# RWKV-6 attention followed by a Hyena gate, last output product split: two blocks of y ahead, the third behind

## The chip, the cores and the metric

One core of one Trainium2 chip. Times are device microseconds. The engines are PE (matrix products), VectorE (DVE), ScalarE (ACT), GpSimd (POOL) and SyncE (SP), which here only issues DMAs; sixteen DMA engines move the data. A PE product is two instructions in the profile, a weight load (PEld) and a matmul.

## The reference

Two layers in a row, for 4 batches, 768 time steps, 8 heads of 48 (384 channels):

```
# 1: a decaying state per head
y[t]  = r[t] @ (state + (u * k[t]) outer v[t])
state = w[t] * state + k[t] outer v[t]
# 2: x = y with the heads side by side, [batch, 768, 384]
x1, x2, x3 = split(x @ w_proj)
conv = irfft(rfft(x2, time) * rfft(filter, time))
out  = (x1 * conv * x3) @ w_out
```

## The kernel before, in words

Layer 1 is done in 24 chunks of 128 time steps, six for each batch. Layer 2 is done batch by batch: the projections, a Fourier transform written as matrix products, a pointwise product with the filter's transform, the inverse transform, the gate, and the output product.

The order of the work is written out by hand. ORDER is a text of words such as `P:po.3.3@2`: the engine (P is PE, V VectorE, A ScalarE, G GpSimd, S SP), the operation with its arguments (here batch 3, tile 3), and after the @ the PSUM bank. `emit` calls `op_<name>` for each word. Within an engine, instructions go in the order of the words; between engines, only data, buffers and the marks (!) order them. There are six banks of 128 x 384 fp32 (0 to 5), and one wide one (8). A word that names a bank takes it anew (`ps`) and so waits for the last reader of what lay in it.

What the change touches is the end of each batch:

- The 384 channels are three blocks of 128 (`cb`, CB = 3), with channels on the partitions and the 768 time steps along the row. For each block the inverse transform gives two halves, which VectorE adds and subtracts into `SD_b[cb]` (`op_s` line 759, `op_d` line 768).
- `op_gm` (line 692) makes a half of the gate x1 * x3, `op_gc` copies a half of the third projection out of PSUM (line 241), `op_x1` one of the first.
- `op_yy` (line 771) multiplies: y[:, cb, :] = SD[cb] * g[:, cb, :], 128 x 768 in bf16, on VectorE or GpSimd. All three blocks lie in one tile, `y_b[0]`, the same one for all batches.
- `op_po` (line 776) is the output product for one tile of 128 time steps: three matmuls, one for each block of y, summed in one PSUM bank. There are six tiles for a batch.
- `op_o` evicts the bank into `o_b` (line 241 on ScalarE, 242 on VectorE; the tile is called `filt` in odd batches), and `op_st` (line 785) has SP store the 192 KB to HBM.

In the last batch there is nothing left beside this. The words after the last projections are: `yy.3.2` on GpSimd, then on VectorE `yy.3.0`, `gm.3.1.1`, `yy.3.1`, so block 1 is the last to be ready. PE's six `po` words follow, in banks 2, 3, 0, 2, 3, 0, with five evictions on ScalarE and one (`o.3.1`) on VectorE. The stores go in the order 3, 5, 4, 2, 0, 1.

Of the kernel before, what the change touches and what calls it, by code (L numbers as in the profile page):

```python
# [19 lines left out]
B, H, S, D = 4, 8, 768, 48  # L20
# [3 lines left out]
CB = C // L  # L24
# [104 lines left out]
S:st.2.5 V:pp.3.2 P:po.2.4@1 S:st.2.1 V:pp.3.1 P:p1.3.2.1@0 V:o.2.4 P:i2.3.2@2 V:g.3.0.1 S:st.2.4  # L129
P:i1.3.2@1 A:ec.3.2 V:x1.3.2.1 P:p3.3.2.1@3 V:d.3.2 P:i2.3.0@0 V:s.3.2 P:i1.3.0@2 A:ec.3.0 V:g.3.2.1  # L130
P:i2.3.1@1 V:s.3.0 G:yy.3.2! P:i1.3.1@3 A:ec.3.1 V:d.3.0 P:p1.3.1.1@0 V:s.3.1 P:p3.3.1.1@2
A:x1.3.1.1 V:d.3.1 A:gc.3.1.1 V:yy.3.0 V:gm.3.1.1 V:yy.3.1 P:po.3.3@2 P:po.3.5@3 A:o.3.3 P:po.3.4@0
A:o.3.5 S:st.3.3 P:po.3.2@2 A:o.3.4 S:st.3.5 P:po.3.1@3 A:o.3.2 S:st.3.4 P:po.3.0@0 V:o.3.1 S:st.3.2
A:o.3.0 S:st.3.0 S:st.3.1
"""


# [1 line left out]
def kernel(  # L139
# [90 lines left out]
    bank_of = {}  # L230

    def ps(name, bank, shape=(L, C), dt=FP32):
        t = (wide if bank == 8 else banks[bank]).tile(
            list(shape), dt, tag="a", name=name.replace(".", "_")
        )
        bank_of[name] = t
        return t
# [532 lines left out]
    def op_yy(e, b, cb):  # L770
        return two(e).tensor_mul(y_b[0][:, cb, :], SD_b[cb], g_b[b % 2][:, cb, :])  # L771

    def op_po(e, b, ti, bank):
        p = ps(f"po.{b}.{ti}", bank)
        for cb in range(CB):
            nc.tensor.matmul(  # L776
                p, y_b[0][:, cb, ti * L:(ti + 1) * L], wout[:, cb, :],
                start=(cb == 0), stop=(cb == CB - 1),
            )

    def op_o(e, b, ti):
        copy(e, o_b[b % 2][:, ti, :], bank_of[f"po.{b}.{ti}"])
# [101 lines left out]
```

## Time and profile before

| | |
|---|---|
| median of 3 runs | 159.45 us (159.06 to 159.55) |
| the profiled execution's own time | 159.7 us |
| its span, first to last instruction | 158.0 us |
| mean granted PE clock | 0.993 |
| PE, VectorE, ScalarE, GpSimd busy | 93%, 90%, 79%, 71% |
| stores of the last batch | 6 of 192 KB, issued from 151.57 to 154.84 |

All times in the text are microseconds from the start of the span. A row of the timeline gives the start, the duration, the engine and line, the operation, what it writes and reads, its count, and in brackets how long the engine stood idle before it and what ended that. SPq is the queue of SP: its duration is the time that SP is taken up with issuing, and not that of the transfer. A group's row gives durations in ns as least, median and most. A window's row gives each engine's busy time and instructions, then PE's clock, the busy share of the 16 DMA engines, and the GB/s that they moved.

### The profile page before, as it was taken

The numbers are of one execution on the slowest core, as the hardware profiler recorded it, in microseconds if no ns is written. First come the engines' busy times: TensorE is split into PE (matmuls) and PEld (weight loads), VectorE is DVE, ScalarE is ACT, GpSimd is POOL, SyncE is SP. The second block draws the span as 40 slices with busy tenths as digits, with TensorE's granted clock in tenths as the row PEclk, the third lists the DMA queues.
The fourth block names the chain that finished last, engine by engine and source line by source line (L and its number), as shares of the span: only waits on it lengthen the run. The fifth ranks groups of instructions, "written<-read, shape, count | busy, mean of one in ns | idle before, by whom it ended". The sixth has DMA issues, their size and how long they took to land.

```text
span 158.0 us, 4363 instructions
## 1 busy us (share of the span) xinstructions
PE 146.7 (93%) x1635; PEld 96.9 (61%) x1638; DVE 142.1 (90%) x287; ACT 125.6 (79%) x264; POOL 111.7 (71%) x136
## 2 busy tenths in 40 slices
PE   6999999989999999999999999999999989899770
PEld 6656467666567676767566766666667746456340
DVE  6989999985999999999998999999999999899920
ACT  4699799998889999999979999799786755644460
POOL 7373399987767888987797479887988969741400
PEclk9999999999999999999999999999999999999997
DMA  5999999999999989979899989999972000016026
GB/s 104 206 245 260 181 217 190 173 257 167 279 228 222 217 174 193 269 152 220 166 191 217 194 172 224 290 215 204 223 212 71 0 0 4 2 52 244 5 77 228
DMA packets 105704, 27.43 MB, mean 174 GB/s; under 512 B 100305, under 2 KB 105682, under 8 KB 105682
## 3 DMA queue, kind: packets, MB, share of 16 engines
q1 hardware_dynamic: 105682, 27.14, 76.9%
q8 instruction: 13, 0.21, 0.6%
q14 instruction: 9, 0.07, 0.1%
HBM read 22.41 MB, written 4.72 MB: 172 GB/s over the span
## 4 chain that ended last, share of the span: by engine, by line
PE 61%; ACT 11%; DVE 9%; POOL 8%; DMA 6%; issue 2%; SPq 0%; POOLq 0%; ACTq 0%
PE p L666 12%; PE po L776 8%; DMA ldw<-in_w_dram 6%; PE x L697 5%; PE i L737 5%; PE tqk L566 4%; PE f L411 4%; PE sc L579 3%; PE cs L467 2%; PE ce L473 2%; PE f L404 2%; PE y L622 2%; ACT F L344 2%; POOL vc L560 2%; POOL T L444 1%
## 5 line engine op out<-in xcount | busy, mean ns | idle before, releaser
L586 DVE TENSOR_TENSOR mt<-sc,mask_excl 128x1024 bf16<-128x1024 f32 x24 | 29.2, 1215 | 0.5 <-PE sc L579 0.5
L666 PE MATMUL p<-xT,wproj 128*128 128x384 bf16 x144 | 29.3, 326 | 0.3 <-ACT xT L241 0.2
L528 POOL TENSOR_TENSOR rk<-ldr,ldk 128x384 bf16<-128x384 f32 x23 | 22.9, 999 | 6.4 <-DMA ldr<-in_r_dram 2.5
L560 POOL TENSOR_TENSOR vc<-v,cc 128x384 bf16<-128x384 bf16 x24 | 20.0, 836 | 6.1 <-DVE cc L534 1.8
L241 ACT ACTIVATE qkT<-tqk 128x1024 bf16<-128x1024 bf16 x20 | 20.5, 1032 | 3.8 <-PE tqk L566 3.8
L666 PEld LDWEIGHTS <-wproj 128*128 128x128 bf16 x144 | 13.0, 98 | 7.1 <-issue 0.3
L697 PE MATMUL x<-wproj,sd 128*128 128x384 bf16 x72 | 14.8, 326 | 1.4 <-DVE sd L653 1.1
L463 ACT ACTIVATE lg<-ldw 128x384 bf16<-128x384 f32 x24 | 12.7, 529 | 3.4 <-DMA ldw<-in_w_dram 3.2
L776 PE MATMUL po<-wout,y 128*128 128x384 bf16 x72 | 13.7, 326 | 1.2 <-DVE y L771 1.2
L566 PE MATMUL tqk<-ident,qk 128*128 128x128 bf16 x192 | 14.6, 219 | 0.1
L771 POOL TENSOR_TENSOR y<-SD,g 128x768 bf16<-128x768 bf16 x6 | 9.9, 1642 | 6.6 <-DVE g L682 4.6
L525 POOL TENSOR_TENSOR qk<-ldr,eq 128x384 bf16<-128x384 f32 x12 | 12.3, 1027 | 2.9 <-ACT eq L492 1.2
L737 PE MATMUL i<-m_b,P 128*128 128x384 bf16 x72 | 13.8, 326 | 0.3 <-DVE g L682 0.3
L566 PEld LDWEIGHTS <-qk 128*128 128x128 bf16 x192 | 11.6, 98 | 3.3 <-DVE qk L509 0.7
L241 ACT ACTIVATE ab<-x 128x384 bf16<-128x384 f32 x22 | 10.8, 497 | 3.0 <-PE x L697 3.0
L731 POOL TENSOR_TENSOR P<-UA,UB 128x768 bf16<-128x768 bf16 x5 | 8.2, 1641 | 4.5 <-DVE UB L722 2.8
L521 POOL TENSOR_TENSOR qk<-ldk,en 128x384 bf16<-128x384 f32 x10 | 10.0, 1000 | 1.9 <-DVE qk L525 1.1
L605 DVE TENSOR_TENSOR S<-kv,eq 128x384 bf16<-128x384 f32 x20 | 11.0, 549 | 0.2
L241 ACT ACTIVATE x<-p 128x384 bf16<-128x384 f32 x21 | 9.9, 496 | 1.5 <-PE p L666 1.5
L776 PEld LDWEIGHTS <-y 128*128 128x128 bf16 x72 | 6.5, 98 | 5.9 <-DVE y L771 2.0
L242 POOL CAST v<-ldv 128x384 bf16<-128x384 f32 x12 | 6.5, 547 | 5.1 <-DVE UA L393 4.6
L634 DVE TENSOR_TENSOR xn<-y,vc 128x384 bf16<-128x384 f32 x18 | 9.9, 548 | 0.0
(155 smaller groups left out, 411.7 us busy)
## 6 DMA issues: line engine op xcount, KB each, us to landing
ldw<-in_w_dram SPq DMA_DIRECT2D x24, 192.0 KB, 3.8
ldk<-in_k_dram SPq DMA_DIRECT2D x24, 192.0 KB, 4.0
ldr<-in_r_dram SPq DMA_DIRECT2D x24, 192.0 KB, 4.1
ldv<-in_v_dram SPq DMA_DIRECT2D x24, 192.0 KB, 4.1
out_dram<-o SPq DMA_DIRECT2D x12, 192.0 KB, 3.2
out_dram<-filt SPq DMA_DIRECT2D x12, 192.0 KB, 2.2
o<-in_moe_w_proj_dram SPq DMA_DIRECT2D x3, 576.0 KB, 5.4
filt<-in_moe_filter_fft_dram SPq DMA_DIRECT2D x1, 1152.0 KB, 7.2
```

The source lines that it names most:

```text
L241: return nc.scalar.activation(out=o, in_=i, func=AF.Copy)
L463: nc.scalar.activation(out=lg_b[c % 3][:, :, 0:D], in_=ld["w"][c % LD], func=AF.Ln)
L525: return two(e).tensor_mul(qk_b[c % 3][:, 0, :, 0:D], ld["r"][c % LD], eq)
L528: return two(e).tensor_mul(rk_b[c % 2], ld["r"][c % LD], ld["k"][c % LD])
L560: return two(e).tensor_mul(vc_b[c % 3], v_b[c % 4], cc_b[c % 3].to_broadcast([L, H, D]))
L566: nc.tensor.transpose(p[:, x, j, :], qk_b[c % 3][:, x, 2 * j:2 * j + 2, :], ident)
L586: nc.vector.tensor_mul(mt_b[c % 3], bank_of[f"sc{c}"].rearrange("p q j t -> p (q j) t"), dataclasses.replace(m[:, :], ap=[m[:, :].ap[0], [ ...
L605: nc.vector.tensor_mul(S_b[nth(c)], bank_of[f"kv{c}"], ph.to_broadcast([L, HP, 2, D]))
L666: nc.tensor.matmul(p, wproj[:, n, cb, fb * L:(fb + 1) * L], xT_b[b % 2][:, cb, sl], start=(cb == 0), stop=(cb == CB - 1),)
L697: nc.tensor.matmul(p, sd_b[q][:, cb, ti * L:(ti + 1) * L], wproj[:, 1, cb, :], start=(cb == 0), stop=(cb == CB - 1),)
L737: nc.tensor.matmul(p, P_b[b % 2][:, s // 2, s % 2, cb * L:(cb + 1) * L], m_b[:, s].rearrange("p a t -> p (a t)"), start=(i == 0), stop=(i ...
L776: nc.tensor.matmul(p, y_b[0][:, cb, ti * L:(ti + 1) * L], wout[:, cb, :], start=(cb == 0), stop=(cb == CB - 1),)
```

## The change

The three matmuls of an output tile are now taken in the order of blocks 2, 0, 1, in all batches. For the last batch the product of a tile is two words: `poa` takes a bank and issues the matmuls of blocks 2 and 0, `pob` issues that of block 1 into the same bank. The `poa` of tiles 3, 5 and 4 stand ahead of `yy.3.1` in the list and ahead of all `pob` on PE; the other three tiles have `poa` and `pob` next to each other. The six tiles take the banks 4, 5, 0, 1, 3, 2. The evictions and the stores keep their engines and their order, and are moved to the end of the list.

```diff
-A:x1.3.1.1 V:d.3.1 A:gc.3.1.1 V:yy.3.0 V:gm.3.1.1 V:yy.3.1 P:po.3.3@2 P:po.3.5@3 A:o.3.3 P:po.3.4@0
-A:o.3.5 S:st.3.3 P:po.3.2@2 A:o.3.4 S:st.3.5 P:po.3.1@3 A:o.3.2 S:st.3.4 P:po.3.0@0 V:o.3.1 S:st.3.2
-A:o.3.0 S:st.3.0 S:st.3.1
+A:x1.3.1.1 V:d.3.1 A:gc.3.1.1 V:yy.3.0 V:gm.3.1.1 P:poa.3.3@4 P:poa.3.5@5 P:poa.3.4@0 V:yy.3.1
+P:pob.3.3 A:o.3.3 P:pob.3.5 A:o.3.5 P:pob.3.4 A:o.3.4 P:poa.3.2@1 P:pob.3.2 A:o.3.2 P:poa.3.1@3
+P:pob.3.1 V:o.3.1 P:poa.3.0@2 P:pob.3.0 A:o.3.0 S:st.3.3 S:st.3.5 S:st.3.4 S:st.3.2 S:st.3.0
+S:st.3.1
...
-    def op_po(e, b, ti, bank):
-        p = ps(f"po.{b}.{ti}", bank)
-        for cb in range(CB):
+    FIRST = (2, 0, 1)
+
+    def po(b, ti, cbs):
+        p = bank_of[f"po.{b}.{ti}"]
+        for cb in cbs:
             nc.tensor.matmul(
                 p, y_b[0][:, cb, ti * L:(ti + 1) * L], wout[:, cb, :],
-                start=(cb == 0), stop=(cb == CB - 1),
-            )
+                start=(cb == FIRST[0]), stop=(cb == FIRST[-1]),
+            )
+
+    def op_po(e, b, ti, bank):
+        ps(f"po.{b}.{ti}", bank)
+        po(b, ti, FIRST)
+
+    def op_poa(e, b, ti, bank):
+        ps(f"po.{b}.{ti}", bank)
+        po(b, ti, FIRST[:2])
+
+    def op_pob(e, b, ti):
+        po(b, ti, FIRST[2:])
```

## The prediction

> **What bounds the kernel now.** I read the page first, then the timeline of the last ten microseconds, then SP's issues and the DMA windows there.
>
> ```profile
> span 158.0 us, 4363 instructions
> PE 146.7 (93%) x1635; PEld 96.9 (61%) x1638; DVE 142.1 (90%) x287; ACT 125.6 (79%) x264; POOL 111.7 (71%) x136
> ...
> PE 61%; ACT 11%; DVE 9%; POOL 8%; DMA 6%; issue 2%; SPq 0%; POOLq 0%; ACTq 0%
> ```
>
> Over the whole span PE and VectorE are nearly full, and the chain runs mostly over PE. The change moves work only behind the last pipeline stage, so the averages say little. What counts is who ends last there. The timeline columns are start, duration, engine, line, operation, tiles, count, and the idle time before it:
>
> ```profile
> 147.35 1.65 POOL L771 TENSOR_TENSOR y<-SD,g 128x768 bf16<-128x768 bf16 x1 [4.58 <-DVE g L682]
> ...
> 147.81 1.14 PE L666 MATMUL p<-xT,wproj 128*128 128x384 bf16 x6
> ...
> 149.02 0.55 DVE L771 TENSOR_TENSOR y<-SD,g 128x768 bf16<-128x768 bf16 x1
> 149.51 0.36 DVE L692 TENSOR_TENSOR g<-g,x 128x384 bf16<-128x384 bf16 x1
> ...
> 149.63 0.34 PE L776 MATMUL po<-wout,y 128*128 128x384 bf16 x1 [0.68 <-DVE y L771]
> 149.90 0.56 DVE L771 TENSOR_TENSOR y<-SD,g 128x768 bf16<-128x768 bf16 x1
> ...
> 150.52 2.94 PE L776 MATMUL po<-wout,y 128*128 128x384 bf16 x17 [0.56 <-DVE y L771]
> 151.05 1.95 ACT L241 ACTIVATE filt<-po 128x384 f32<-128x384 f32 x4 [1.58 <-PE po L776]
> ...
> 153.00 0.56 DVE L242 COPY filt<-po 128x384 f32<-128x384 f32 x1 [2.54 <-PE po L776]
> 153.49 0.49 ACT L241 ACTIVATE filt<-po 128x384 f32<-128x384 f32 x1 [0.48 <-PE po L776]
> ```
>
> The three blocks of y arrive as block 2 (POOL, 149.00), block 0 (149.57), block 1 (150.46). PE takes them as 0, 1, 2 within each of six tiles, so it gets one matmul done at 149.63 and stands until 150.52. The other 17 leave at (2.94 - 0.326)/16 = 0.163 us each, 0.326 being what one matmul takes in the trace:
>
> ```profile
> L776 PE MATMUL po<-wout,y x18: 326/326/337, 149.6 to 153.1; 128*128 128x384 bf16 x18
> ```
>
> Evictions follow at 1.95/4 = 0.488 us on ScalarE, and the last one ends at 153.98. But the span ends at 158.0, four microseconds later, so the stores must be read too:
>
> ```profile
> 151.57 0.33 SPq L785 DMA_DIRECT2D out_dram<-filt  x1
> ...
> 152.06 1.23 SPq L785 DMA_DIRECT2D out_dram<-filt  x1
> ...
> 153.38 0.87 SPq L785 DMA_DIRECT2D out_dram<-filt  x2
> ...
> 154.34 0.91 SPq L785 DMA_DIRECT2D out_dram<-filt  x2
> ```
>
> SP issues the first store 0.03 us after its eviction. The second issue holds SP for 1.23 us instead of 0.33, until 153.29; the third, whose tile was ready at about 152.52, goes at 153.38. The windows (the last two columns are the share of the 16 DMA engines and GB/s) show what that costs:
>
> ```profile
> 152.25:152.50 0.25, 0.25 (x4) 0.12 (x3) 0.00 (x0) 0.25 (x1) 0.00 (x0) 1.00 0.32 117
> 152.25:153.00 0.75, 0.75 (x7) 0.43 (x6) 0.00 (x0) 0.75 (x2) 0.00 (x0) 1.00 0.68 246
> 153.00:153.75 0.75, 0.46 (x3) 0.07 (x1) 0.56 (x1) 0.27 (x2) 0.00 (x0) 1.00 0.10 27
> 153.75:156.50 2.75, 0.00 (x0) 0.00 (x0) 0.00 (x0) 0.23 (x1) 0.00 (x0) 0.85 0.99 355
> 156.50:158.00 1.50, 0.00 (x0) 0.00 (x0) 0.00 (x0) 0.00 (x0) 0.00 (x0) 0.50 0.02 5
> ```
>
> The first store's data flows from about 152.42 (a third of the first window at the full rate), 0.85 us after its issue. From 153.00 to 153.75 the DMA engines stand almost idle. From 153.75 all 16 are full until 156.50, with five stores: 2.75/5 = 0.55 us each. Then 1.5 us of landing and closing. So the last stage is bound by the stores: five in a row, starting when SP is let go of the second.
>
> Why was SP held? The DMA view of 151.5 to 152.0, in 40 slices, shows one packet, an instruction fetch on queue q8; the third line is the page's count of such fetches:
>
> ```profile
> GB/s 0 0 0 0 1311 0 0 0 0 0 0 0 0 0 0 0 0 0 0 0 0 0 0 0 0 0 0 0 0 0 0 0 0 0 0 0 0 0 0 0
> ...
> q8 instruction: 1, 0.02, 17.0%
> ...
> q8 instruction: 13, 0.21, 0.6%
> ```
>
> It starts in the fifth slice, 151.55, just before the first store, and takes 17% of 16 engines in 0.5 us, which on one engine is 0.17 x 16 x 0.5 = 1.36 us, to 152.91. The second issue ends 0.38 us behind that. The 0.10 of the engines busy after 153.00 is little more than one engine of 16 (0.06), which fits one engine doing its part of the first store late. Thirteen fetches over 1635 + 1638 records make one per 252 matmuls and weight loads: I read q8 as PE's own instruction stream, fetched by PE's progress. That reading is an inference.
>
> **The change part by part.**
>
> *Order of blocks (2, 0, 1), all batches.* Same 72 matmuls. Only a stall on y could change, and in the list of waits PE's output product waits for y twice in all, both in the rows above:
>
> ```profile
> PE po L776 <- DVE y L771: 1.2, 2, 0.7
> ```
>
> So batches 0 to 2 are costed at nothing: PE's earlier work covers y there, and if that cover were thinner the new order would wait no later than the old, since every order ends with the last block.
>
> *Six matmuls ahead.* Block 2 of the first tile can go at about 149.05, when POOL and PE's preceding product (147.81 + 1.14 = 148.95) are done. Block 0 goes at 149.63 as now, and four more behind it: the sixth has left by 149.63 + 5 x 0.163 = 150.44. Block 1 still comes at 150.46, so the next matmul goes at 150.52 as now, with 0.08 us of standing in place of 0.56. Then 12 are left instead of 17: PE ends 5 x 0.163 = 0.81 us sooner, at 152.65 instead of 153.46.
>
> *Banks.* The six tiles lie in six banks instead of reusing three, and banks 4 and 5 must be free. Bank 5's last reader before is VectorE's product on f.3.2, bank 4's comes ahead of it in VectorE's order; the last readers of the others are ScalarE's:
>
> ```profile
> 141.57 0.96 DVE L725 TENSOR_TENSOR UA<-f,T 128x768 bf16<-128x768 f32 x1
> ...
> 148.56 0.49 ACT L241 ACTIVATE x<-p 128x384 bf16<-128x384 f32 x1 [0.54 <-PE p L666]
> 148.99 0.49 ACT L241 ACTIVATE g<-p 128x384 bf16<-128x384 f32 x1
> ```
>
> All are done before 149.5, and bank 2 (the g row) is taken only by the last tile: no wait added.
>
> *Evictions.* The first needs one matmul after block 1 instead of two: 151.05 - 0.16 = 150.89. ScalarE then runs without a gap, because PE is ahead of it: four by 150.89 + 1.95 = 152.84, the last 152.84 to 153.33, against 153.98. So 0.65 of PE's 0.81 arrives here; ScalarE has become late next. VectorE's one eviction (ninth matmul after 150.52) ends at about 152.75, ahead of its store.
>
> *Stores.* Same six, same order on SP; nothing is moved past them. The first issue goes at 151.57 - 0.16 = 151.41, its data at 152.26. If SP is not held, issues follow every 0.49 us and data every 0.55, so the engines never run dry: 152.26 + 6 x 0.55 = 155.56 against 156.50, a gain of 0.94. If SP is held exactly as now, only 0.16.
>
> *The fetch.* At 151.55 PE has started its eighth matmul (150.52 + 6 x 0.163 = 151.50). With the change the eighth goes at 150.52 + 0.16 = 150.68, so the fetch moves to about 150.73 and ends at 152.09. The second issue comes at 151.90; with the same 0.38 behind the fetch it ends at 152.47, its data starts 0.46 later (as 153.29 to 153.75) at 152.93, and five stores end at 155.68: gain 0.82. Free of it 0.94. There is a smaller fetch in the window from 153.5 to 154.0:
>
> ```profile
> q14 instruction: 1, 0.01, 4.7%
> ```
>
> That is 0.047 x 16 x 0.5 = 0.37 us on one engine, so far partly inside the idle stretch. If it now falls among the full stores it costs up to 0.37; nothing if its engine has slack. I keep 0.45 to 0.94 and take 0.8, near the upper end, since the rows give 0.82 and only part of the small fetch is new.
>
> The Trainium skill (Runtime: NRT & Kernel Launch, Instruction fetch mechanics) says that instructions come in blocks of 16 KiB, 256 instructions, and that crossing such a block is mostly hidden. The size agrees with 0.21 MB in 13 fetches; were the cost hidden here too, the hold would have another cause and the first rival below would hold. The Trainium skill (DMA: Bandwidth & Descriptors, Queues, rings and completion order) says that a DMA engine changes queues only at packet boundaries; by that rule one 16 KB packet blocks its engine for its whole 1.36 us, as the thin stretch after 153.00 suggests.
>
> Sum: the profiled execution took 159.7 with a span of 158.0; 0.8 less is 158.9. The median of the three runs is 0.25 below that execution, so I forecast 159.45 - 0.8 = 158.65.
>
> **The rivals.**
>
> *The hold stays.* If the 1.23 us belong to the second store and not to the fetch, or the fetch does not follow PE, SP is held as now and the gain is the 0.16 of the first eviction: 159.3. In between, a fetch that moves by half as much leaves 0.3 to 0.5. For it: one instance only. Against it: six stores of the batch before had no such issue,
>
> ```profile
> L785 SPq DMA_DIRECT2D out_dram<-o x6: 332/332/341, 140.5 to 144.8; - x6
> ```
>
> 332 to 341 ns, each. Chance 0.24.
>
> *No head start.* If the write of block 1 is made to wait for the six reads of the same tile of y, it runs from about 150.65 (150.28 + 0.33 and a semaphore) to 151.21, the first eviction comes at about 151.63, 0.58 later than now. PE's eighth matmul then goes at about 151.43, and with its fetch 0.07 sooner than now SP is let go 0.07 sooner: 159.4. Against it: the matmul at 149.63 read block 0 of that tile 0.83 us before block 1 was written, so blocks are told apart at least in that direction. Chance 0.07.
>
> *The fetch lands among the stores: slower.* The place of the fetch goes by a count of instructions, and the new waits may shift that count. Ten matmuls further on, behind the last of the 18 (152.32), it would block one engine for 1.36 us in the full stretch. That engine ends at 155.56 + 1.36 = 156.92, 0.42 behind now: 159.87. It decides as soon as more than 0.94 of the 1.36 fall behind 152.26. Against it: the matmuls and loads are as many as before, so ten matmuls, 20 instructions, would have to vanish. Chance 0.05.
>
> **How the numbers follow.** Forecast 0.64, and the rivals 0.24, 0.07 and 0.05. A measurement of this kernel can tell about 0.3%, 0.48 us, from no change. Faster: nearly all of the forecast (0.62) and the upper part of the first rival (0.04), 0.66. Slower: 0.05. Same: 0.29. The forecast alone reaches from 158.5 to 159.0; with 0.15 for the spread of the runs below, and the first rival above, the range is 158.35 to 159.4, which leaves out the slower case and part of the second rival.
>
> **What would show it.** Right: one matmul of the output product near 149.05, five from 149.63, twelve from 150.52; ScalarE's five evictions in one piece from 150.89; the q8 fetch near 150.7; all SP issues below 0.6 us; DMA engines full from 152.3 to 155.6 without a gap. Wrong: an issue above 1 us again with the fetch elsewhere (first rival); a VectorE write of y that starts after 150.6 (second); the fetch behind 152 (third).

## The result, and the profile after

| | before | changed |
|---|---|---|
| median of 20 runs each | 160.01 us | 158.62 us |
| ratio, 95% interval | | 0.9946 (0.992 to 0.9971) |
| profiled execution, span | 159.7, 158.0 | 158.6, 156.8 |
| mean granted PE clock | 0.993 | 0.997 |

The kernel is faster by 0.54%, between 0.29 and 0.80%: 0.9 us, with bounds of 0.5 and 1.3. The ratio leaves out the runs that took over 1.5% longer than the fastest of their kernel (of the traced executions, that of the third kernel below is one), so it is not the ratio of the two medians, which are 1.39 us apart. Runs of one kernel spread over more than two microseconds here, so most of what follows goes by the traces of the tail, one execution for each kernel.

The timeline of the changed kernel's end, with the columns as before:

```profile
146.72 1.64 POOL L772 TENSOR_TENSOR y<-SD,g 128x768 bf16<-128x768 bf16 x1 [4.58 <-DVE g L683]
...
148.40 0.55 DVE L772 TENSOR_TENSOR y<-SD,g 128x768 bf16<-128x768 bf16 x1
...
148.42 0.34 PE L780 MATMUL po<-wout,y 128*128 128x384 bf16 x1
...
149.00 3.02 PE L780 MATMUL po<-wout,y 128*128 128x384 bf16 x17 [0.25 <-DVE y L772]
149.28 0.56 DVE L772 TENSOR_TENSOR y<-SD,g 128x768 bf16<-128x768 bf16 x1
...
150.27 2.28 ACT L242 ACTIVATE filt<-po 128x384 f32<-128x384 f32 x5 [1.41 <-PE po L780]
150.78 2.79 SPq L800 DMA_DIRECT2D out_dram<-filt  x6
151.57 0.56 DVE L243 COPY filt<-po 128x384 f32<-128x384 f32 x1 [1.73 <-PE po L780]
```

One matmul goes behind POOL's block 2 and the others from block 0 on. PE stands 0.25 us for block 0 where it stood 0.68. For block 1, where it stood 0.56, it now stands 0.07: its seventh matmul starts at 149.89, 0.23 behind the sixth, and 0.16 is the usual distance. VectorE writes block 1 from 149.28 to 149.84, and doesn't wait for the reads that run beside it. ScalarE's five evictions stand in one row. SP takes 2.79 us for its six issues, where it took 3.68. The stores' group and the windows behind it:

```profile
L800 SPq DMA_DIRECT2D out_dram<-filt x6: 332/398/412, 150.8 to 153.2; - x6
```

```profile
151.75:154.95 3.20, 0.27 (x2) 0.00 (x0) 0.38 (x1) 0.65 (x2) 0.00 (x0) 1.00 0.99 354
155.00:155.50 0.50, 0.00 (x0) 0.00 (x0) 0.00 (x0) 0.00 (x0) 0.00 (x0) 1.00 0.06 22
155.50:156.80 1.30, 0.00 (x0) 0.00 (x0) 0.00 (x0) 0.00 (x0) 0.00 (x0) 0.57 0.00 0
```

No issue is above 0.412 us; the 1.23 us hold is gone, and so is the idle stretch. All 16 DMA engines are full until 154.95. Then the share is 0.06 for half a microsecond: one engine of 16 is late and the other fifteen have finished. The DMA views of 150.0 to 150.5 and of 152.5 to 153.0 tell of two fetches:

```profile
GB/s 0 0 0 0 0 1311 0 0 0 0 0 0 0 0 0 0 0 0 0 0 0 0 0 0 0 0 0 0 0 0 0 0 0 0 0 0 0 0 0 0
...
q8 instruction: 1, 0.02, 12.6%
```

```profile
q14 instruction: 1, 0.01, 3.8%
```

PE's 16 KB fetch now starts in the sixth slice, at 150.06, lasts 0.126 x 16 x 0.5 = 1.01 us and is over before any store's data. The small fetch (0.30 us) now falls into the full stretch.

To compare the kernels I use the **tail**: from the end of VectorE's block 0 of y in the last batch to the end of the span. It is 158.0 - 149.57 = 8.43 us before and 156.8 - 148.95 = 7.85 changed, 0.58 shorter. The other 0.62 by which this span is shorter lies ahead of the tail and is no effect of the change that can be shown: the kernels below differ from these two in a few instructions up to there, and reached that point anywhere between 148.84 and 152.59.

### The profile page after: what moved, and what is told of

The parts are those of the page before. It is cut to its first block, busy times and chain, and to the rows that moved or that the text cites. A ratio compares the mean times of both kernels' runs of the same rounds, so it can differ in the third digit from the quotient of the medians.

```text
span 156.8 us, 4363 instructions
## 1 busy us (share of the span) xinstructions
PE 146.7 (94%) x1635; PEld 97.0 (62%) x1638; DVE 142.2 (91%) x287; ACT 125.5 (80%) x264; POOL 111.9 (71%) x136
## 4 chain that ended last, share of the span: by engine, by line
PE 64%; DVE 11%; ACT 6%; DMA 6%; POOL 5%; issue 3%; SPq 2%; POOLq 0%; ACTq 0%
PE p L667 11%; PE po L780 8%; PE x L698 6%; PE f L412 5%; PE tqk L567 5%; PE i L738 4%; PE z L812 3%; PE sc L580 3%; DMA ldk<-in_k_dram 3%; DMA ldv<-in_v_dram 3%; PE cs L468 2%; PE f L405 2%; PE ce L474 2%; PE y L623 2%; PE z L807 2%
## 5 line engine op out<-in xcount | busy, mean ns | idle before, releaser
L698 PEld LDWEIGHTS <-sd 128*128 128x128 bf16 x72 | 6.2, 97 | 5.8 <-DVE sd L654 2.0
```

The costliest lines, as they stand in the source:

```text
L698: nc.tensor.matmul(p, sd_b[q][:, cb, ti * L:(ti + 1) * L], wproj[:, 1, cb, :], start=(cb == 0), stop=(cb == CB - 1),)
```

## The experiments

All are read from that tail; "behind block 0" counts from its start. Ratios are against the kernel before on the same chip.

**The order alone.** The kernel before with its blocks in the order 2, 0, 1:

```diff
-        for cb in range(CB):
+        for cb in (2, 0, 1):
-                start=(cb == 0), stop=(cb == CB - 1),
+                start=(cb == 2), stop=(cb == 1),
```

> The kernel before with only the block order 2, 0, 1; no split, old banks, old order of PE. Tail is the time from the end of VectorE's block 0 of y in the last batch to the end of the span: 8.43 us before, 7.85 after the change. Both theories: PE gets two matmuls ahead instead of one, so PE and the first eviction come 0.16 us sooner. Fetch theory (PE's 16 KB instruction fetch goes by PE's progress, blocks one DMA engine and with it SP's next store issue): the fetch starts behind the eighth matmul, 0.16 sooner too, still meets the first store, and SP is held at the second for over 1 us; tail about 8.25. Rival (the hold belongs to the second store): the same hold, the same 8.25. Earlier batches: no change from the order.

Tail 8.06; ratio 0.9958 (0.9915 to 1.0001). PE and the first eviction came as expected, 0.16 sooner, but the hold was gone as well. Two timeline rows, the stores' group, and the DMA view of 150.25 to 150.75:

```profile
149.41 0.49 PE L776 MATMUL po<-wout,y 128*128 128x384 bf16 x2 [0.58 <-ACT g L241]
...
150.39 2.77 PE L776 MATMUL po<-wout,y 128*128 128x384 bf16 x16 [0.50 <-DVE y L771]
```

```profile
L785 SPq DMA_DIRECT2D out_dram<-filt x6: 332/397/440, 151.3 to 154.2; - x6
```

```profile
GB/s 0 0 0 0 0 0 0 0 0 0 0 0 0 0 0 0 0 0 0 0 0 0 0 0 0 1311 0 0 0 0 0 0 0 0 0 0 0 0 0 0
```

Here the second matmul went ahead of PE's wait for block 1, at 149.41 + 0.16 = 149.57, and the fetch began at 150.56, in the 26th slice: 1.0 us later, as before (150.52, 151.55) and changed (149.00, 150.06). So it follows PE's second matmul, and is not tied to the eighth, as I had read it. Counted from block 0 it came 0.87 sooner, enough to miss the stores.

**The fetch moved, nothing else.** The kernel before with `P:zs37@0` for `P:zs29@0`: eight small warm-up matmuls more at the start.

> The kernel before with eight more small warm-up matmuls at its start (16 more PE instructions), nothing else. Fetch theory: PE's last fetch comes eight matmuls sooner, at 150.5 or sooner on the old clock, and is over by 151.9, ahead of the first store's data; no issue on SP above 0.6 us, the gap in the stores' data is gone, and the tail is 0.4 to 0.8 shorter (7.6 to 8.0 instead of 8.43) with PE's end where it was. Rival (the hold belongs to the second store, or the fetch does not go by PE's count): an issue of about 1.2 us again, tail 8.43.

PE's fetch came 1.15 us ahead of the end of block 0, and no issue was held:

```profile
L785 SPq DMA_DIRECT2D out_dram<-filt x6: 332/339/382, 153.1 to 156.0; - x6
```

So the hold belongs to the fetch, and the first rival falls. But the tail was 8.30, only 0.13 shorter, and the ratio 1.0008 (0.9972 to 1.0044). Two limits were right behind. The last eviction still ends 4.41 behind block 0, so the last two stores could not go sooner than 4.44 and 4.86. And one DMA engine ended late again, with the small fetch at 4.03 for 0.93 us:

```profile
155.50:157.40 1.90, 0.00 (x0) 0.00 (x0) 0.00 (x0) 0.06 (x1) 0.00 (x0) 1.00 0.86 313
157.55:158.05 0.50, 0.00 (x0) 0.00 (x0) 0.00 (x0) 0.00 (x0) 0.00 (x0) 0.54 0.07 25
```

The last kernels below tell the two apart: without the small fetch, and with the same last eviction, the gain is 0.62, so the late engine took 0.49 of it.

**The fetch among the stores.** The changed kernel with eight warm-up matmuls fewer (`P:zs21@0`).

> The changed kernel with eight warm-up matmuls fewer at its start (16 fewer PE instructions), nothing else. Fetch theory: the last fetch comes eight matmuls later, about 1.4 us behind the end of block 0 plus 1, that is among the stores; one SP issue is held for 0.5 us or more and one DMA engine runs late: tail 8.3 to 8.9 instead of 7.85, with PE and the evictions as in the changed kernel. This is the rival of the prediction that ends slower, made on purpose. If the fetch does not go by PE's count: tail 7.85.

Tail 8.79, with PE and the evictions as in the changed kernel. Ratio 0.9963 (0.9907 to 1.0019). SP's fourth and sixth issues:

```profile
155.81 0.88 SPq L800 DMA_DIRECT2D out_dram<-filt  x1
...
157.26 1.28 SPq L800 DMA_DIRECT2D out_dram<-filt  x1
```

```profile
157.00:159.25 2.25, 0.00 (x0) 0.00 (x0) 0.00 (x0) 0.00 (x0) 0.00 (x0) 1.00 0.62 218
```

The small fetch began at 155.81 and PE's at 157.20, each with the issue that it held, and the engines were 0.62 busy in the end. The mechanism of the third rival is thus real: fetches among the stores hold SP and leave the engines partly idle. That the kernel ends slower for it is not shown. This tail is 0.36 longer than that of the kernel before, with all of PE's gain kept, but it is that of the one execution traced, and the ratio leans the other way. PE's fetch came later than expected, 4.61 behind block 0 and not 2.4; why it waited is open.

**A longer head start.** Block 1 of y in two halves of the time steps, the first ahead of the last gate product; tiles 0 to 5 in order; block 2 of three tiles first:

```diff
-V:yy.3.0 V:gm.3.1.1 P:poa.3.3@4 P:poa.3.5@5 P:poa.3.4@0 V:yy.3.1
+V:yy.3.0 V:yh.3.1.0 V:gm.3.1.1 V:yh.3.1.1
+P:pc.3.0.2@4 P:pc.3.1.2@5 P:pc.3.2.2@0 P:pc.3.0.0 P:pc.3.1.0 P:pc.3.0.1 A:o.3.0 P:pc.3.1.1 A:o.3.1
...
+    def op_yh(e, b, cb, hf):
+        sl = halves[hf]
+        return two(e).tensor_mul(y_b[0][:, cb, sl], SD_b[cb][:, sl], g_b[b % 2][:, cb, sl])
```

> The changed kernel with block 1 of y written in two halves of the time steps (the first half ahead of the last gate product), the tiles of the first half first (0, 1, 2, 3, 4, 5 through evictions and stores), and block 2 of three tiles ahead of block 0. First eviction about 0.5 us sooner than in the changed kernel. If the stores' data at 0.55 us each bound the end (my theory), the tail shortens by the same 0.5, to about 7.35. If the late DMA engine seen in the changed kernel (one engine ends 0.5 behind the others) sets the end by something tied to the end of PE or ScalarE, less: 7.6 or more.

Tail 7.44, ratio 0.9914 (0.9872 to 0.9956). The first eviction came at 0.76 behind block 0 instead of 1.32, and 0.41 of the 0.56 reached the end. One engine ended late once more, with the small fetch at 2.77, and an issue of 0.71 beside it.

**Whose is the small fetch?** Eight more one-column copies on ScalarE (`A:na8`) or memsets on VectorE (`V:nv8`) at the start of the changed kernel; one execution each.

> The changed kernel with eight one-column copies more on ScalarE at its start, nothing else. Tail (end of block 0 of y to the end of the span) was 7.85 us, with the small fetch of 8 KB at 3.64 behind block 0, among the stores, and one DMA engine ending 0.5 behind the others. Theory A (the small fetch is ScalarE's, by its count of instructions): it moves ahead of the stores by eight ScalarE instructions, to before 1.0, the late engine is gone, tail 7.3 to 7.5. Theory B (another engine's, or tied to the end of the work): the fetch stays at 3.2 to 3.7, tail 7.8 to 7.9.

> The changed kernel with eight small memsets more on VectorE at its start, nothing else. Theory A (the small fetch is ScalarE's): it stays at 3.2 to 3.7 behind block 0, tail 7.8 to 7.9. Theory B (VectorE's, by its count): it moves ahead of the stores, tail 7.3 to 7.5. If neither this nor the ScalarE kernel moves it, it is SyncE's, GpSimd's or tied to the end of the work.

With the copies, the small fetch moved to 0.45 behind block 0, ahead of all stores, and no engine ended late. The view of 150.75 to 151.25 has it alone, in the 14th slice:

```profile
GB/s 0 0 0 0 0 0 0 0 0 0 0 0 0 655 0 0 0 0 0 0 0 0 0 0 0 0 0 0 0 0 0 0 0 0 0 0 0 0 0 0
...
q14 instruction: 1, 0.01, 6.2%
```

With the memsets it stayed among the stores, at 3.25; an issue was held for 0.85, and the tail was 7.96. It is ScalarE's, by its count. The four kernels below that have the copies bear this out: there it comes at 0.45 to 0.49. The tail with the copies was 7.61, above the expected 7.3 to 7.5: this time PE's fetch took 1.40 us (17.5% in the view of 151.5 to 152.0), until 2.59 behind block 0, and the second issue was held.

```profile
152.72 0.71 SPq L810 DMA_DIRECT2D out_dram<-filt  x1
```

**The head start without the small fetch.** The longer head start with both additions.

> The kernel with block 1 of y in two halves (tail 7.44 us, small fetch at 2.77 behind block 0), with the eight ScalarE copies and the eight VectorE memsets more at its start. If the small fetch belongs to one of the two and costs the end the 0.4 to 0.6 by which one DMA engine ends late: no fetch among the stores, tail 6.9 to 7.0. If it stays among them: 7.4.

Tail 6.95, ratio 0.9917 (0.9873 to 0.9961). The tail is 0.49 shorter than with the fetch in the way; the ratio does not resolve that.

**All three with no fetch near the stores.** Eight matmuls (`P:zs37@0`) and eight ScalarE copies more in the kernel before, the changed one, and the one with halves.

> The kernel before with eight warm-up matmuls and eight one-column ScalarE copies more at its start, so that neither fetch should meet the stores. Theory (fetches block a DMA engine each; else the last eviction bounds): no issue above 0.5 us, no late engine, last eviction as before at 4.41 behind block 0, sixth issue at 4.86, landed 1.9 to 2.0 later, tail 7.7 to 7.8 (before 8.43). If the gap came from the stores themselves: 8.3 or more.

> The changed kernel with the same eight matmuls and eight copies more at its start. Theory: stores back to back from 2.67 behind block 0, six at 0.55, tail 7.35 to 7.45 (changed kernel 7.85). Against the clean kernel before, the split alone is then worth 0.3 to 0.4 and not the 0.94 of the forecast's unhindered stores, the rest having been the fetches. Rival: the split alone keeps 0.6 or more.

> The kernel with block 1 of y in two halves and tiles 0 to 5 in order, with the same eight matmuls and eight copies more at its start. Theory: stores back to back from 2.1, tail 6.8 to 6.9 (7.44 with both fetches in the way, 6.95 with PE's fetch close to the first store). It should be the shortest tail of all; against the kernel before about 1.6 us.

Tails 7.81, 7.35 and 6.78; ratios 0.9941 (0.9906 to 0.9976), 0.994 (0.9901 to 0.9979) and 0.9886 (0.9838 to 0.9934). First the kernel before, then the changed one:

```profile
151.75:153.50 1.75, 0.98 (x7) 0.39 (x4) 0.56 (x1) 1.02 (x3) 0.00 (x0) 1.00 1.03 367
...
153.75:155.25 1.50, 0.00 (x0) 0.00 (x0) 0.00 (x0) 0.00 (x0) 0.00 (x0) 0.89 0.78 280
```

```profile
152.00:155.10 3.10, 0.27 (x2) 0.00 (x0) 0.38 (x1) 0.65 (x2) 0.00 (x0) 1.00 1.03 366
155.10:155.25 0.15, 0.00 (x0) 0.00 (x0) 0.00 (x0) 0.00 (x0) 0.00 (x0) 1.00 0.11 31
```

Without fetches the old kernel runs dry after four stores, waiting for the last eviction (0.78 of the engines in the later window). The changed one keeps the engines full from first to last and has no straggler. The third kernel is the best version found.

So the tails split up as follows. The change, with no fetch in the way, is worth 7.81 - 7.35 = 0.46. The fetches cost 8.43 - 7.81 = 0.62 before and 7.85 - 7.35 = 0.50 changed. The gain of 0.58 is 0.46 from the split and 0.12 from fetches that fell better, though not well. The intervals of the three ratios hold what the tails give, but the times do not show the split's part: they are 0.9941 without it and 0.994 with it. So this account rests on the tails. The changed kernel and the one with memsets have the same instructions there, and their tails differ by 0.11, so that the 0.12 is no more than one execution can differ from the next.

## Why the prediction was right, point by point

**Earlier batches at nothing: right as far as can be seen.** The list of waits has the output product waiting for y once in the whole changed kernel, in the tail (the 0.07 is too short for this list):

```profile
PE po L780 <- DVE y L772: 0.2, 1, 0.2
```

**Matmuls ahead, banks: right.** The last matmul starts 2.75 behind block 0 instead of 3.56: 0.81, as forecast. The second rival is out: block 1 is written while matmuls read the same tile. One detail was misread: bank 3's last reader is VectorE, in `op_d`, and not ScalarE; it is done at 149.11 before, early enough.

**Evictions: a term mis-sized.** The first came 0.16 sooner, as forecast, but the last ended 0.81 sooner (3.60 instead of 4.41), not 0.65. The step that failed is "ScalarE has become late next": the 0.488 us between evictions that I took for ScalarE's pace was PE's, three matmuls of 0.163. With tiles waiting, ScalarE starts one every 0.37 us (1.32, 1.71, 2.08, 2.45 behind block 0), and it stood 0.15 before the last one, waiting for PE. The kernel with memsets has the first four in a row of their own, 1.64 us where the kernel before took 1.95:

```profile
150.64 1.64 ACT L242 ACTIVATE filt<-po 128x384 f32<-128x384 f32 x4 [1.42 <-PE po L780]
```

**Stores: right for fifteen engines.** Their data ended at 6.00 behind block 0 (154.95) against 6.93 (156.50): 0.93, forecast 0.94.

**PE's fetch: mechanism right, place misread.** It moved out of the stores' way and took the hold with it. It follows the second matmul and not the eighth, so it moved by 0.87 rather than 0.82; here that made little difference. The forecast's second issue, held to 152.47, was not held, and that was luck in part: the fetch took 1.01 us in this execution and not 1.36. In the kernel with copies, whose instructions in the tail are the same, it took 1.40, and the second issue was held for 0.71.

**The small fetch: the term that ate the rest.** I bounded it at 0.37 and, in taking 0.8, left it little. Among full stores it cost about 0.5, the time by which one engine ended late, and more than the 0.30 that the fetch itself took. The forecast therefore stood at 0.8 where the tail gave 0.58.

**The total.** The measured 0.9 (0.5 to 1.3) holds both. That 158.62 lies next to the forecast 158.65 is partly luck: the forecast started from 159.45, and the kernel before, measured with it, came to 160.01.

**What I had wrong about the share of the parts.** I let the hold decide: 0.94 without it, 0.16 with it. The second kernel shows that removing the hold alone gives 0.13, because ScalarE's fetch then makes one engine late. With that fetch moved too, the old order gives 0.62 and is bound by its last eviction. The split adds 0.46 to that.

The Trainium skill (Runtime: NRT & Kernel Launch, Instruction fetch mechanics) has the cost of crossing an instruction block as mostly hidden. PE's matmuls agree: they start every 0.163 us while its fetch runs in the kernel before. What is not hidden is what the fetches do to the stores: together they cost 0.62 us of the tail before and 0.50 changed. The Trainium skill (DMA: Bandwidth & Descriptors, Queues, rings and completion order) has each DMA engine change queues only at packet boundaries. The traces fit that: where the small fetch falls among full stores, one engine of 16 ends late, 0.06 of the share in the changed kernel and 0.07 in the second one.

## What to carry to other kernels

When the last stage ends in stores, follow the chain to the last landing: PE's end moved by 0.81 us here and the tail by 0.58. Before calling a cause the bound, ask what is next behind it: freeing SP alone gave 0.13, since another fetch then made one engine late, and behind that stood the last eviction. And check where instruction fetches fall in the trace's DMA view; a few small instructions at the start of an engine's stream move them.

## What the runs showed of the hardware that was not expected

- PE's fetch of 16 KB took 0.96 to 1.40 us on one engine in the tails of these kernels. In the seven kernels with PE's stream unshifted it began 0.87 to 1.13 us behind PE's second matmul of the last output product, while the DMA engines were idle. In the third kernel it began at 4.61 behind block 0, with stores queued.
- ScalarE's 8 KB fetch took 0.31 to 0.93 us in the tails. Among full stores one engine then ended about 0.3 to 0.5 us behind the others.
- Nine of SP's issues were held while such a fetch ran, for 0.44 to 1.28 us; the others took 0.33 to 0.42. Six held issues ended 0.37 to 0.38 us behind the end of PE's fetch, and three 0.13 behind that of ScalarE's. Not every issue beside a fetch was held: in the second kernel two went out during ScalarE's, at 0.33 and 0.38. That the store before it must first get through the blocked engine is an inference.
